# First block of x in column slices, each turned on TensorE just ahead of its products

## The chip, the cores and the metric

One core of one Trainium2 chip. The metric is the device time of one execution in microseconds (us). The kernel before took 542.69 us (median of 3 runs, 542.49 to 542.8). The question of the whole document is about the first 35 us of it: what follows is not touched by the change.

Names: TensorE (PE in the profile, with its weight loads as PEld), VectorE (DVE), ScalarE (ACT), GpSimd (POOL), SyncE's queue of transfers (SPq). "Turn" means a 128x128 transpose on TensorE through the identity matrix. Where turns stand between products, a "turn" is one call of `turn`: eight such transposes in the kernel before, four in the changed one. "Eviction" is the copy of a finished PSUM bank to SBUF. At "half pace" a matmul of 512 columns starts 0.427 us after the one before it instead of 0.216 (both in the profile of the kernel before); "release" is the moment when half pace ends. A "filler" is a matmul of zeros whose result nobody uses.

## The reference

```python
B, S, Dm, Df = 1, 2048, 1024, 3584          # all bf16
g = einsum("bsd,df->bsf", x, w_gate)
u = einsum("bsd,df->bsf", x, w_up)
h = gelu(g) * u                             # tanh form
out = einsum("bsf,fd->bsd", h, w_down)
```

## The kernel before

The kernel keeps x transposed (`xT`, k on the partitions) in blocks of 512 rows, handles two blocks per pass, and multiplies 256 columns of `w_gate` and `w_up` at a time. For most of its length it uses seven products instead of eight per pair of blocks, made from sums and differences of tiles: `s` of weights, `t` of `xT`. VectorE makes the first of these. Only the first block (block 0) of the first pass with the first 256 weight columns is multiplied plainly, while `s` and `t` do not exist yet. The change touches this beginning alone.

How block 0 is loaded and turned, and the order of the transfers, all of them on one queue:

```python
def load_x(c):                       # four tiles of 128 rows, 2048-byte rows
    for i in range(NS):              # NS = 4
        xn = slot([P, Dm], bf16, "xn")
        nc.sync.dma_start(out=xn, in_=x2[r0 : r0 + P, :])
...
def turn(xT, xn, c, i, copy):        # 8 transposes into one bank, one eviction
    tp = bank[4 + i].bitcast(bf16).rearrange("p (k r) -> p k r", k=NKB)
    for ko in range(NKB):            # NKB = 8
        nc.tensor.transpose(tp[:, ko, :], xn[i][:, ko * P : (ko + 1) * P], ident)
    copy(out=xT[c][:, :, i * P : (i + 1) * P], in_=tp)
...
xn0 = load_x(0)
for k0, k1 in ((0, 2), (2, 5), (5, NKB)):
    load_wf(nc.sync, k0, k1)         # first weights, gate then up, three parts
w = load_w(1)                        # next weights, gate then up
for ko in range(NKB):
    transposing(xT, 1, ko, N)        # second block, transposed by the transfer
ahead = load_w(2)
```

What the engines do with it:

```python
keep_warm(NWARM, N)                  # 5 matmuls of zeros, 512 columns
for i in range(NS):
    if i > 0:
        keep_warm(3, 2 * P)          # 3 fillers of 256 columns
    turn(xT, xn0, 0, i, on_act if i == 1 else on_dve)
plain(bank[0:4], 0, range(0, 2), parts=2)
plain(bank[0:4], 0, range(2, NKB))   # pairs of k-blocks: per pair, bank by bank
s["s1"] = s["how"]["s1"](s, range(1))
finish(bank[0:4], 0)                 # twice: h = gelu(gate bank) * up bank
s["s1"] += s["how"]["s1"](s, range(1, 2))
nxt = {"p1": first_product(odd, xT, w)}
s.make("sa", "s2", "s3", "s4")       # VectorE goes on without a pause ...
t.make("t1")                         # ... into the differences of xT
```

`plain` makes four results (gate and up, twice 128 columns) in four PSUM banks. It takes two k-blocks for one bank, then two for the next. `finish` needs a Gelu on ScalarE and a product `hT` on VectorE for each half.

## Time and profile before

| what | value | where it is read |
|---|---|---|
| time (median), span of the profiled run (which took 542.47 us) | 542.69 us, 540.6 us | times, page |
| TensorE busy | 535.9 us, 99% | page, part 1 |
| first turn, first product | 3.53, 7.18 us | timeline |
| first chunk (block 0) ends | 14.18 us | records of single matmuls |
| VectorE's second `hT` product starts | 14.57 us | timeline |
| last TensorE wait for VectorE | 29.15 us | timeline |

From the page of the kernel before: the span, the busy line of TensorE (busy us, share, instructions) and the chain that ended last.

```profile
span 540.6 us, 7439 instructions
PE 535.9 (99%) x2414; PEld 378.8 (70%) x2414; DVE 341.4 (63%) x526; ACT 258.7 (48%) x463; POOL 236.4 (44%) x213
...
PE 99%; ACT 0%; DVE 0%; issue 0%
```

The timeline of the kernel before, with lines left out. Columns: start in us, duration in us, engine, line, operation, output<-inputs, shape, count, and in brackets the idle time before it and what ended that.

```profile
1.19 2.31 PE L501 MATMUL bank<-warm 128*128 128x512 bf16 x5 [1.19 <-DVE warm L432]
...
3.53 1.03 PE L448 MATMUL bank<-ident,xn 128*128 128x128 bf16 x8
4.35 0.85 PE L501 MATMUL bank<-warm 128*128 128x256 bf16 x3
4.99 0.80 PE L448 MATMUL bank<-ident,xn 128*128 128x128 bf16 x8
...
6.74 0.61 PE L448 MATMUL bank<-ident,xn 128*128 128x128 bf16 x8
7.18 17.52 PE L111 MATMUL bank<-xT,w 128*128 128x256 bf16 x88
...
13.08 0.60 ACT L179 ACTIVATE g<-bank 128x512 f32<-128x512 f32 x1 [4.93 <-PE bank L111]
13.71 0.69 DVE L90 TENSOR_TENSOR hT<-g,bank 128x512 bf16<-128x512 f32 x1 [1.02 <-ACT g L179]
13.94 0.60 ACT L179 ACTIVATE g<-bank 128x512 f32<-128x512 f32 x1 [0.27 <-PE bank L111]
14.57 0.69 DVE L90 TENSOR_TENSOR hT<-g,bank 128x512 bf16<-128x512 f32 x1 [0.18 <-ACT g L179]
15.18 0.68 DVE L90 TENSOR_TENSOR s<-w 128x512 fp32r<-128x512 bf16 x1
```

Two things to see. The turns at 3.53 take 1.03 us for eight, those at 6.74 take 0.61: TensorE runs at half pace until about 5.4 us. And from 15.18 on VectorE's lines have no bracket, so it never waits again in this stretch; each of its instructions starts when the one before lets it.

The same timeline further on: TensorE's last waits in this kernel that VectorE ends.

```profile
27.34 1.46 PEld L111 LDWEIGHTS bank<-t,s 128*128 128x128 f32 x7 [0.31 <-DVE hT L90]
27.80 1.29 DVE L90 TENSOR_TENSOR t<-xT 128x512 fp32r<-128x512 bf16 x2
...
29.15 0.99 PEld L111 LDWEIGHTS bank<-t,s 128*128 128x128 f32 x5 [0.35 <-DVE t L90]
```

The two differences `t` started at 27.80 end at 29.09, and TensorE goes on at 29.15. After that it has no wait that matters: whatever the beginning gains or loses by here stays to the end.

### The profile page before, as it was taken

To read this page: it belongs to the slowest core of one execution; us is meant where nothing else is said; L and a number is where in the kernel's file an instruction comes from. 1 tells how busy PE (TensorE), PEld (TensorE's weight loads), DVE (VectorE), ACT (ScalarE), POOL (GpSimd) and SP (SyncE) were. 2 spreads that over 40 slices of the span, in tenths; PEclk is the share of its full clock that TensorE was granted. 3 is DMA by queue.
4 is the path that set the end of the run, shared out by engine and by line. 5 is a ranking of instruction groups with operands and counts; after the bars stand their busy time and mean duration, and the time that the engine had idled before them with its cause. 6 is when DMAs were issued, how large, how long until landed. Compare 5 with 4: busy or idle time off the path is not lost.

```text
span 540.6 us, 7439 instructions
## 1 busy us (share of the span) xinstructions
PE 535.9 (99%) x2414; PEld 378.8 (70%) x2414; DVE 341.4 (63%) x526; ACT 258.7 (48%) x463; POOL 236.4 (44%) x213
## 2 busy tenths in 40 slices
PE   9999999999999999999999999999999999999997
PEld 5567777667766646888876776677777775488885
DVE  2986666776666895694945545555544559676730
ACT  2566666566665410255355555555555541114431
POOL 0069966677774400000097777777766600000000
PEclk9999999999999999999999999999999999999999
DMA  9776666666654899979672222222331069363751
GB/s 245 152 187 176 175 183 203 190 185 199 200 165 171 269 381 313 295 189 294 230 194 79 78 79 78 79 78 80 84 100 50 1 196 384 140 236 95 231 188 49
DMA packets 108133, 93.28 MB, mean 173 GB/s; under 512 B 17216, under 2 KB 92992, under 8 KB 108096
## 3 DMA queue, kind: packets, MB, share of 16 engines
q1 hardware_dynamic: 108096, 92.82, 59.2%
q8 instruction: 19, 0.31, 0.3%
q14 instruction: 18, 0.15, 0.1%
HBM read 74.45 MB, written 15.20 MB: 166 GB/s over the span
## 4 chain that ended last, share of the span: by engine, by line
PE 99%; ACT 0%; DVE 0%; issue 0%
PE bank L111 98%; PE bank L501 1%; PE bank L448 0%; ACT st L412 0%; DVE warm L432 0%
## 5 line engine op out<-in xcount | busy, mean ns | idle before, releaser
L93 POOL TENSOR_TENSOR s<-w 128x512 fp32r<-128x512 bf16 x100 | 116.9, 1189 | 154.9 <-PE bank L111 154.9
L111 PE MATMUL bank<-t,s 128*128 128x512 f32 x648 | 157.4, 398 | 0.0
L111 PEld LDWEIGHTS bank<-t,s 128*128 128x128 f32 x648 | 121.6, 188 | 28.2 <-DVE t L90 0.3
L111 PE MATMUL bank<-xT,w 128*128 128x512 bf16 (+1 forms) x504 | 116.2, 377 | 0.0
L107 ACT COPY p<-bank 128x512 f32<-128x512 f32 x124 | 70.5, 591 | 94.0 <-PE bank L111 94.0
L90 DVE TENSOR_TENSOR hT<-g,bank 128x512 bf16<-128x512 f32 x112 | 76.6, 687 | 55.1 <-ACT g L179 49.5
L111 PEld LDWEIGHTS <-w 128*128 128x128 bf16 x504 | 45.1, 98 | 59.0 <-issue 13.4
L90 DVE TENSOR_TENSOR sum<-bank,p 128x512 f32<-128x512 f32 x54 | 37.4, 692 | 52.6 <-PE bank L111 50.9
L179 ACT ACTIVATE g<-sum 128x512 f32<-128x512 f32 x81 | 51.5, 636 | 34.5 <-DVE sum L90 33.6
L111 PE MATMUL bank<-q 128*128 128x512 f32 x240 | 58.9, 389 | 0.0
L111 PE MATMUL bank<-t,sa 128*128 128x512 f32 x216 | 58.6, 413 | 0.0
L93 POOL TENSOR_TENSOR s<-w,s 128x512 fp32r<-128x512 bf16 x50 | 57.7, 1175 | 0.0
L93 POOL TENSOR_TENSOR s<-s,w 128x512 fp32r<-128x512 f32 x50 | 57.0, 1161 | 0.0
L111 PE MATMUL bank<-tb,s 128*128 128x512 f32 x216 | 53.3, 389 | 0.0
L111 PEld LDWEIGHTS bank<-q 128*128 128x128 f32 x240 | 45.1, 188 | 9.3
L111 PE MATMUL bank<-raw,hT 128*128 128x512 bf16 x224 | 48.7, 379 | 0.0
L111 PEld LDWEIGHTS bank<-t,sa 128*128 128x128 f32 x216 | 40.7, 188 | 10.6
L111 PEld LDWEIGHTS bank<-tb,s 128*128 128x128 f32 x216 | 40.6, 188 | 8.4
L102 ACT CAST tb<-raw 128x512 fp32r<-128x512 bf16 x28 | 17.2, 626 | 59.6 <-DMA raw<-in_w_down_dram 24.2
L107 ACT COPY u<-bank 128x512 f32<-128x512 f32 x62 | 35.9, 590 | 19.7 <-PE bank L111 19.7
L90 DVE TENSOR_TENSOR bank<-bank,p 128x512 f32<-128x512 f32 x54 | 37.8, 700 | 8.9 <-PE bank L111 5.8
L90 DVE TENSOR_TENSOR q<-hT 128x512 fp32r<-128x512 bf16 x56 | 38.5, 687 | 4.7 <-PE bank L111 4.7
(45 smaller groups left out, 444.7 us busy)
## 6 DMA issues: line engine op xcount, KB each, us to landing
raw<-in_w_down_dram SPq DMA_DIRECT2D x80, 256.0 KB, 4.8
q<-td SPq DMA_DIRECT2D x60, 256.0 KB, 5.0
w<-in_w_gate_dram SPq DMA_DIRECT2D x27, 512.0 KB, 5.9
w<-in_w_up_dram SPq DMA_DIRECT2D x27, 512.0 KB, 7.0
td<-m SPq DMA_DIRECT2D x12, 768.0 KB, 4.6
w<-td SPq DMA_DIRECT2D x6, 1024.0 KB, 9.5
out_dram<-st SPq DMA_DIRECT2D x32, 128.0 KB, 1.7
td<-w SPq DMA_DIRECT2D x2, 768.0 KB, 7.0
```

The source lines that it names most:

```text
L90: nc.vector.tensor_tensor(out=out, in0=a, in1=b, op=op)
L93: nc.gpsimd.tensor_tensor(out=out, in0=a, in1=b, op=op)
L102: nc.scalar.copy(out=t, in_=src)
L107: nc.scalar.copy(out=t, in_=ps)
L111: nc.tensor.matmul(ps, lhsT=lhs, rhs=rhs, start=start, stop=stop, skip_group_check=True)
L179: nc.scalar.activation(g, src, ACT.Gelu_apprx_tanh)
L501: nc.tensor.matmul(bank[3][:, :cols], lhsT=warm[:, :P], rhs=warm[:, :cols], start=True, stop=True)
```

## The change

Intent: do not wait for the whole of block 0. Load it in four slices of 256 columns (two k-blocks each, 512-byte rows), put the first weights between the slices, and turn each k-block just ahead of the four matmuls that use it. Those matmuls keep TensorE busy, so the fillers go.

```diff
-    def load_x(c):  ... out=xn, in_=x2[r0 : r0 + P, :]
+    def load_x(q):
+        xn = slot([P, NS, 2 * P], bf16, "xn")
+        cols = x2[:N, 2 * q * P : 2 * (q + 1) * P]
+        nc.sync.dma_start(out=xn, in_=cols.rearrange("(i p) c -> p i c", p=P))
+        return xn
+
+    def turn(k):
+        tp = bank[4 + k % 4].bitcast(bf16)[:, :N]
         for i in range(NS):
-    ... 8 transposes of one row tile, eviction of 128x1024 by VectorE or ScalarE
+            nc.tensor.transpose(tp[:, i * P : (i + 1) * P],
+                xn0[k // 2][:, i, k % 2 * P : (k % 2 + 1) * P], ident)
+        nc.vector.tensor_copy(out=xT[0][:, k, :], in_=tp)
...
+    ORDER_0 = "T0 T1 M0 M1 T2 T3 M2 T4 M3 T5 M4 T6 M5 T7 M6 M7"   # turns, products
-    xn0 = load_x(0)
-    for k0, k1 in ((0, 2), (2, 5), (5, NKB)):
-        load_wf(nc.sync, k0, k1)
+    xn0 = [load_x(0)]
+    load_wf(0, 2)
+    xn0.append(load_x(1))
+    load_wf(2, 5)
+    xn0 += [load_x(2), load_x(3)]
+    load_wf(5, NKB)
...
-        keep_warm(NWARM, N)
-        for i in range(NS):
-            if i > 0:
-                keep_warm(3, 2 * P)
-            turn(xT, xn0, 0, i, on_act if i == 1 else on_dve)
-        plain(bank[0:4], 0, range(0, 2), parts=2)
-        plain(bank[0:4], 0, range(2, NKB))
+        for _ in range(NWARM):
+            nc.tensor.matmul(bank[3], lhsT=warm[:, :P], rhs=warm, start=True, stop=True)
+        for what, k in ORDER_0:
+            if what == "T":
+                turn(k)
+            else:
+                plain(bank[0:4], 0, [k])        # one k-block over the four banks
```

More of the change, by code (lines that the diff above doesn't have):

```diff
@@ L434 @@
     make_identity(nc, ident)
-    def load_x(c):
-        t = []
-        for i in range(NS):
-            xn = slot([P, Dm], bf16, "xn")
-            r0 = c * N + i * P
-            nc.sync.dma_start(out=xn, in_=x2[r0 : r0 + P, :])
-            t.append(xn)
-        return t
-    def turn(xT, xn, c, i, copy):
-        tp = bank[4 + i].bitcast(bf16).rearrange("p (k r) -> p k r", k=NKB)
-        for ko in range(NKB):
-            nc.tensor.transpose(tp[:, ko, :], xn[i][:, ko * P : (ko + 1) * P], ident)
-        copy(out=xT[c][:, :, i * P : (i + 1) * P], in_=tp)
+    def load_x(q):
[5 more added lines that the diff above has]
+        tp = bank[4 + k % 4].bitcast(bf16)[:, :N]
+        for i in range(NS):
+            nc.tensor.transpose(
+                tp[:, i * P : (i + 1) * P],
+                xn0[k // 2][:, i, k % 2 * P : (k % 2 + 1) * P],
+                ident,
+            )
+        nc.vector.tensor_copy(out=xT[0][:, k, :], in_=tp)
     def transposing(xT, c, ko, r0):
@@ L454, in transposing, with load_wf @@
         )
-    def load_wf(queue, k0, k1):
+    def load_wf(k0, k1):
         for i, src in enumerate((w_gate, w_up)):
-            got = queue.dma_start(
+            nc.sync.dma_start(
                 out=wf[:, i, k0:k1],
@@ L463, in load_wf @@
             )
-            if queue is not nc.sync:
-                tc.keep_in_program_order(got)
+    ORDER_0 = [(step[0], int(step[1])) for step in "T0 T1 M0 M1 T2 T3 M2 T4 M3 T5 M4 T6 M5 T7 M6 M7".split()]
     xT = new_x()
-    xn0 = load_x(0)
     wf = wpool.tile([P, 2, NKB, 2 * P], bf16, name="w")
-    for k0, k1 in ((0, 2), (2, 5), (5, NKB)):
-        load_wf(nc.sync, k0, k1)
+    xn0 = [load_x(0)]
[4 more added lines that the diff above has]
+    load_wf(5, NKB)
     w = load_w(1)
@@ L475, with plain @@
     ahead = load_w(2)
-    def plain(ps, c, kos, parts=1):
-        n = N // parts
-        for k in range(kos.start, kos.stop, 2):
-            for part in range(parts):
-                cols = slice(part * n, (part + 1) * n)
-                for p, (j, i) in zip(ps, [(j, i) for j in range(2) for i in range(2)]):
-                    for ko in (k, k + 1):
-                        matmul(
-                            p[:, cols],
-                            wf[:, i, ko, j * P : (j + 1) * P],
-                            xT[c][:, ko, cols],
-                            ko == 0 and part == 0,
-                            ko == NKB - 1,
-                        )
+    def plain(ps, c, kos):
+        for p, (j, i) in zip(ps, [(j, i) for j in range(2) for i in range(2)]):
+            for ko in kos:
+                matmul(
+                    p,
+                    wf[:, i, ko, j * P : (j + 1) * P],
+                    xT[c][:, ko, :],
+                    ko == 0,
+                    ko == NKB - 1,
+                )
     def finish(ps, c):
@@ L494, in finish @@
             times(j, c, gelu(ps[2 * j]), ps[2 * j + 1])
-    on_dve, on_act = nc.vector.tensor_copy, nc.scalar.copy
     s, t = sums_s(w, dve), sums_t(xT)
     with tc.manual_schedule(engines={ENG.Activation}):
-        def keep_warm(n, cols):
-            for _ in range(n):
-                nc.tensor.matmul(
-                    bank[3][:, :cols], lhsT=warm[:, :P], rhs=warm[:, :cols], start=True, stop=True
-                )
-        keep_warm(NWARM, N)
-        for i in range(NS):
-            if i > 0:
-                keep_warm(3, 2 * P)
-            turn(xT, xn0, 0, i, on_act if i == 1 else on_dve)
-        plain(bank[0:4], 0, range(0, 2), parts=2)
-        plain(bank[0:4], 0, range(2, NKB))
+        for _ in range(NWARM):
[5 more added lines that the diff above has]
+                plain(bank[0:4], 0, [k])
         s["s1"] = s["how"]["s1"](s, range(1))
@@ L522, in rest_of_0 @@
         if part == 0:
-            plain(bank[4:8], 1, range(NKB))
+            for k in range(0, NKB, 2):
+                plain(bank[4:8], 1, (k, k + 1))
             t.make("t2", "tb")
```

## The prediction

> **What bounds the kernel now.** TensorE: busy 535.9 of 540.6 us, 99% of the chain that ended last. In the timeline no gap over 0.1 us follows about 29.5 us, so the change can only win what TensorE is ahead when that steady stream starts. Before it:
>
> - Weights and x share one DMA stream: by the windows view about 310 GB/s from 2 to 8 us.
> - The timeline has warm-up matmuls from 1.19 us, four turns of x between 3.53 and 7.18 with filler matmuls between them, then the first products, gapless from 7.18 to 14.18.
> - VectorE is full (windows view: 2.00 of every 2 us) from 15.2 to 35 us. TensorE waits for it at 27.35 and 29.15 (a difference tile "t" that ended at 29.10). That second wait is the last one: VectorE's chain sets the start of the steady stream.
> - The DMA-transposed rows of the second x block land at about 18.45 (4th) up to 22.82 us (8th); TensorE first uses the 8th at 23.03. Slack 0.2 us.
>
> **Removed.** 9 filler matmuls (3 x 0.32 cold, 6 x 0.11 warm, 1.6 us), one ScalarE copy (1.01 us) and an activation-table load, and the wait for all of x before the first product.
>
> **Added and moved.** Transposes stay 32 (0.107 us apart cold, 0.055 warm). VectorE evicts 8 times 128x512 instead of 3 times 128x1024 (0.69 each); my estimate from that duration is 0.40 each. The first product needs slice 0, the first weights and an eviction: estimated 4.7-4.9 us instead of 7.2. But products now wait for data: two turns then their product leaves an eviction gap of about 0.45 us near 7 us, and the fifth product waits for the last weights. Product time itself (32 x 0.216 = 6.9 us) is unchanged.
>
> Slices have 512-byte rows, not 2048. In the DMA packet records of this trace a 512 B packet takes 27 ns and a 2048 B one 84 ns: 19 against 24 GB/s per engine. [...]this trace shows it is slower than 2 KB. Estimate: x takes 0.5 us longer, so the last weights land near 10.7 (10.2 before), and everything queued behind, including the 8th transposed row (to about 23.3), is later by up to 0.5.
>
> So the eight steps end at about 13.8 instead of 14.18: 0.4 us. Then the gain goes: all four banks now finish within the last 0.86 us, so Gelu of bank 0 (0.60) holds the next product by 0.2, and both Gelus run after it, so VectorE's second h product starts near 14.6, as before (14.58). Its full chain then ends as before, and the transposed rows cap TensorE as well. **Little or nothing remains at 29 us.**
>
> **Risk.** [...] Here half pace lasts to about 5.4 us. [...]
>
> **Predicted: 542.8 us, range 541.9 to 544.3.** Faster by over 2%: 1%; within 2%: 98%; slower: 1%.
>
> **Right if:** first product near 4.8, first chunk done 13.5-14.0, VectorE's chain from 15.2 unchanged within 0.3 us, TensorE after 30 us shifted under 0.3 us. **Wrong if:** matmuls keep a 0.43 us pitch past 6 us (clock; slower), or the second x block lands at the old times and the head gains over 0.7 us (then up to 0.5 faster), or slices land more than 1 us late.

The forecast's sum: 0.4 us gained at the end of the chunk (13.8 instead of 14.18), all of it lost again to the late Gelus, so about the time of the kernel before, 542.8 us. Beside the sum stood a risk term, one chance in four that half pace lasts longer without fillers and the beginning loses time. The range, up to 544.3, leaves room for it; the sum does not hold it.

## The result, and the profile after

The changed kernel took 543.62 us (median of 4 runs, 542.74 to 544.72), the kernel before 542.75 us (4 runs, 542.49 to 542.87). The ratio is 1.0018, with a 95% interval of 0.9994 to 1.0041: the same within 2%, and not clear of noise. Here and below a ratio is the mean time of one kernel's runs over that of the other's runs of the same rounds, so it is not quite the ratio of the medians.

The four times are two pairs: 542.74 and 542.86, 544.37 and 544.72. The profile is of the slowest of them. Its page:

```profile
span 542.9 us, 7407 instructions
PE 537.2 (99%) x2397; PEld 377.5 (70%) x2397; DVE 342.7 (63%) x531; ACT 256.1 (47%) x461; POOL 236.9 (44%) x213
...
PE 98%; DMA 1%; DVE 1%; SPq 0%; ACT 0%; issue 0%
```

The timeline of the changed kernel, same columns, lines left out:

```profile
3.63 1.03 PE L445 MATMUL bank<-ident,xn 128*128 128x128 bf16 x8
...
4.75 0.59 PE L111 MATMUL bank<-xT,w 128*128 128x512 bf16 x1
...
5.99 3.17 PE L111 MATMUL bank<-xT,w 128*128 128x512 bf16 x7 [0.65 <-DMA w<-in_w_up_dram]
...
8.95 1.06 PE L445 MATMUL bank<-ident,xn 128*128 128x128 bf16 x8
...
10.10 1.02 PE L111 MATMUL bank<-xT,w 128*128 128x512 bf16 x4
...
14.44 12.45 PE L111 MATMUL bank<-xT,w 128*128 128x512 bf16 x56
...
15.72 1.09 ACT L179 ACTIVATE g<-bank 128x512 f32<-128x512 f32 x2 [13.71 <-PE bank L111]
16.35 1.28 DVE L90 TENSOR_TENSOR hT<-g,bank 128x512 bf16<-128x512 f32 x2 [0.69 <-PE bank L111]
17.55 0.69 DVE L90 TENSOR_TENSOR s<-w 128x512 fp32r<-128x512 bf16 x1
```

The first product starts 2.4 us sooner than before (4.75 against 7.18), does one matmul, and then TensorE stands until the first up weights have landed at 5.95 us (landing records). The seven matmuls from 5.99 take 3.17 us and the eight turns from 8.95 take 1.06: half pace still, where before it had ended at 5.4. The four matmuls at 10.10 are the first at full pace (0.215 us from start to start). The first chunk ends at 16.17 us, and the second `hT` product, the second of the pair that starts at 16.35, starts at 16.96 in the records instead of 14.58.

Further on the changed kernel shows the same two lines as before, 2.4 us later. Nothing between 15 and 31 us has taken back or added anything:

```profile
30.18 1.29 DVE L90 TENSOR_TENSOR t<-xT 128x512 fp32r<-128x512 bf16 x2
...
31.52 0.99 PEld L111 LDWEIGHTS bank<-t,s 128*128 128x128 f32 x5 [0.33 <-DVE t L90]
```

**Where the head start went, in TensorE's time.** The 32 products take 6.9 us at full pace in both kernels. In this profile 4.75 + 6.9 would be 11.65. To that come 2.47 us because the first eight products took from 4.75 to 8.95 (half pace and the wait for up weights) instead of 1.73; 0.85 for two turns at half pace and 0.89 for four at full pace, all of which now stand between products; and 0.30 for an eviction ahead of the third product. The sum is 16.16, the measured end 16.17.

**A rule that the profiles obey.** The span follows the start of VectorE's second `hT` product. Span minus that start is 526.0 us before (540.57 - 14.58) and 526.0 after (542.94 - 16.96). The experiments add twelve more profiles: eleven lie between 525.9 and 526.1, and one, at 526.3, is told below.

**The clock's own record.** Each trace also keeps, though no view prints it, when the full clock was granted to TensorE: from 5.38 us in the kernel before, from 10.10 in the changed kernel. The grant lasts 535.892 us before and 532.479 us after. In the profiles of the experiments it begins anywhere from 3.92 us (experiment 11) to 9.2 us (experiment 1). What sets its beginning, the traces do not show.

### The profile page after: what moved, and what is told of

It is laid out like the page before. It is cut to its first block, busy times and chain, and to the rows that moved or that the text cites. A ratio compares the mean times of both kernels' runs of the same rounds, so it can differ in the third digit from the quotient of the medians.

```text
span 542.9 us, 7407 instructions
## 1 busy us (share of the span) xinstructions
PE 537.2 (99%) x2397; PEld 377.5 (70%) x2397; DVE 342.7 (63%) x531; ACT 256.1 (47%) x461; POOL 236.9 (44%) x213
## 4 chain that ended last, share of the span: by engine, by line
PE 98%; DMA 1%; DVE 1%; SPq 0%; ACT 0%; issue 0%
PE bank L111 97%; DMA w<-in_w_up_dram 1%; PE bank L445 0%; DVE t L90 0%; DVE bank L90 0%; DVE hT L90 0%; ACT st L412 0%; SPq L459 0%; SPq L439 0%; DVE xT L450 0%
## 5 line engine op out<-in xcount | busy, mean ns | idle before, releaser
L111 PE MATMUL bank<-xT,w 128*128 128x512 bf16 x496 | 118.9, 384 | 0.9 <-DMA w<-in_w_up_dram 0.7
```

Of the source, the lines that this page charges most:

```text
L111: nc.tensor.matmul(ps, lhsT=lhs, rhs=rhs, start=start, stop=stop, skip_group_check=True)
```

## The experiments

Two theories for the two groups of times. *Theory A (clock)*: TensorE starts at half pace, and in some runs of the changed kernel the release comes late, as in its profile (10.10 us against 5.38), because TensorE now stands waiting in that stretch. *Theory B (loads)*: the slow runs are those whose first weights land late, whatever the pace. Beside these stand the smaller claims of the prediction: short rows, the late Gelus, the cap by the second block.

Kernels 1 to 4 ran on one chip, 5 to 8 on a second, 9 to 12 on a third, each with its own runs of the kernel before: medians 542.84 (11 runs, 542.3 to 543.38), 542.61 (11 runs, 542.3 to 543.48) and 542.96 (9 runs, 542.08 to 543.16).

### 1. The changed kernel again

No edit.

> The changed kernel once more, unedited, to see whether its times really fall into two groups (542.74 and 542.86 against 544.37 and 544.72). Theory A (clock): TensorE stays at half pace (0.43 us from one 512-column matmul to the next) until about 10 us in the slow runs[...]; expect two groups again, about 542.8 and 544.5, and in the profile a half pace to about 10 us if the profiled run is over 544, to about 5.4 to 6.8 us if it is under 543. Theory B (loads): the slow runs are those in which the first weights land late (5.95 us in the profile of after); expect two groups that follow the landing of the first up weights, at whatever clock.

Measured: 542.63, 542.92, 543.09 and 544.46, 544.57, 544.77; ratio 1.0013 (0.9999 to 1.0026). Two groups again. Of the ten runs of the changed kernel so far five average 542.85 and five 544.58, which is 1.73 us apart. All ten average 543.71, the 15 runs of the kernel before beside them 542.80, so the mean loss of 0.9 us is that of the slow group. The profile fell on a run of 544.57: half pace until 9.2 us, up weights landed at 5.85 us, second `hT` at 16.78. Both theories expected two groups. Both slow profiles have the late landing and the late release together, so this run does not part the theories.

### 2. Fillers ahead of the first product

```diff
+                if k == 0:
+                    for _ in range(6):
+                        nc.tensor.matmul(bank[3][:, :256], lhsT=warm[:, :P],
+                            rhs=warm[:, :256], start=True, stop=True)
                 plain(bank[0:4], 0, [k])
```

> The changed kernel with six filler matmuls of 256 columns between the first two turns and the first product, about 1.3 us at half pace. Theory A (clock): release near 5.4 us in every run, one group at 542.4 to 542.9, none over 543.2. Theory B (loads): the weights land as late as without fillers, so two groups remain, 542.8 and 544.5.

Measured: 543.13 to 543.79 in five runs, ratio 1.0012 (1.0 to 1.0024). One group, so the slow one is gone, as theory A said, though fillers cannot bring weights sooner. The level that theory A gave, 542.4 to 542.9, was missed by 0.7 us: the fillers themselves hold the first product until 5.79 us, and in this profile the release came only at about 6.9 us.

### 3. The kernel before without its fillers

```diff
         for i in range(NS):
-            if i > 0:
-                keep_warm(3, 2 * P)
             turn(xT, xn0, 0, i, on_act if i == 1 else on_dve)
```

> The kernel before without its nine filler matmuls between the turns, nothing else. Theory A (clock): the first products start at half pace in some or all runs; release moves from 5.4 us to as late as about 10 us, and the time rises by 0.5 to 1.7 us, to 543.2 to 544.4. Theory B (loads): fillers do not matter, 542.4 to 542.9.

Measured: 542.21 us, 541.79 to 542.35, ratio 0.9987 (0.9975 to 0.9999). Neither theory had expected it to be faster. Timeline of this kernel:

```profile
3.49 3.54 PE L448 MATMUL bank<-ident,xn 128*128 128x128 bf16 x32
...
6.87 10.40 PE L111 MATMUL bank<-xT,w 128*128 128x256 bf16 x54
```

The 32 turns run back to back, 3.5 to 6.87, all but the last at 0.107 us from one to the next, that is at half pace, and the first product behind them runs at full pace. The grant of the full clock begins at 6.84, after 3.35 us of nothing but transposes (the five warm-up matmuls end at 3.50). Without the fillers the first product starts 0.3 us sooner than before. Experiment 9 repeats this kernel.

### 4. The kernel before with x in column slices

```diff
-            xn = slot([P, Dm], bf16, "xn")
-            nc.sync.dma_start(out=xn, in_=x2[r0 : r0 + P, :])
+            xn = slot([P, NS, 2 * P], bf16, "xn")
+            cols = x2[:N, 2 * q * P : 2 * (q + 1) * P]
+            nc.sync.dma_start(out=xn, in_=cols.rearrange("(i p) c -> p i c", p=P))
```

(All four slices ahead of all weights, turned slice by slice, fillers kept.)

> The kernel before with x loaded in four slices of 256 columns (512-byte rows) ahead of all weights, turned slice by slice with the fillers kept: the cost of the short rows alone. By the prediction the last of the first weights lands about 0.5 us later than 10.2 us and the 8th transposed row about 0.5 us later than 22.8; TensorE's slack there was 0.2 us, so the time should be 542.7 to 543.3. If the short rows cost nothing, 542.5 to 542.9 and unchanged landings.

Measured: 543.25 us, 542.86 to 543.35, ratio 1.0005 (0.9993 to 1.0017). In the timing alone this is not clear of noise. In the profile the first up weights land at 8.01 us (7.32 before), the last of the first weights at 10.72 (10.20 before), and the first product starts at 7.61 (7.18 before); the second `hT` follows at 15.17, 0.59 later. The eighth row of the second block lands at 22.87 against 22.82. The short rows thus cost about half a microsecond between these two profiles, as predicted, but through the first weights and not through the second block. The sign is safer than the size: in the five profiles with the loads of the kernel before (before, experiments 3, 5, 9 and 12) the first up weights land anywhere from 6.67 to 7.80 us and the last first weights from 9.74 to 10.46, and experiment 4 is later than all five.

### 5. The kernel before with its last k-blocks one by one

```diff
-        plain(bank[0:4], 0, range(2, NKB))
+        plain(bank[0:4], 0, range(2, 6))
+        for ko in (6, 7):
+            for p, (j, i) in zip(bank[0:4], [(j, i) for j in range(2) for i in range(2)]):
+                matmul(p, wf[:, i, ko, j * P : (j + 1) * P], xT[0][:, ko, :],
+                       False, ko == NKB - 1)
```

> The kernel before, with the last two of its eight k-blocks of the first chunk done one by one over the four banks instead of as a pair per bank; same loads, same matmuls. The Gelu theory of the prediction: the banks then finish within 0.86 us instead of 1.5, both Gelus (0.60 each) follow the last products, and VectorE's second h product starts about 0.8 us after the chunk's end instead of 0.4; the time rises by 0.3 to 0.4 us, to about 543.1 to 543.3. Rival (TensorE alone counts): the chunk ends at the same moment, so no change, within 0.1 us of before.

Measured: 543.16 us, 542.58 to 543.46, ratio 1.0009 (0.9996 to 1.0022). Timing again leans the expected way without being clear. The profile decides: the chunk ended at 13.87 us, and the second `hT`, the second of the two below, started at 14.66, which is 0.79 later. Before it was 14.58 - 14.18 = 0.40.

```profile
13.42 1.08 ACT L179 ACTIVATE g<-bank 128x512 f32<-128x512 f32 x2 [5.58 <-PE bank L111]
14.05 1.28 DVE L90 TENSOR_TENSOR hT<-g,bank 128x512 bf16<-128x512 f32 x2 [1.45 <-PE bank L111]
```

The two Gelus run as one stretch because both banks were ready, where before there was a pause of 0.27 us between them that TensorE ended. Banks that finish together cost 0.39 us against banks that finish in turn. The span sides with VectorE and not with TensorE: the chunk ended 0.30 us sooner than in the profile before, the second `hT` started 0.08 later, and the span is 0.12 longer (540.69 against 540.57).

### 6. Fillers inside the wait

```diff
+            if n == 1:                       # after the first matmul of M0
+                for _ in range(fill):        # fill = 4 for M0, else 0
+                    nc.tensor.matmul(bank[3][:, :256], lhsT=warm[:, :P],
+                        rhs=warm[:, :256], start=True, stop=True)
```

> The changed kernel with four fillers of 256 columns placed after the first matmul of the first product, where TensorE waits for the first up weights anyway. Theory A (clock): the slow group near 544.5 vanishes and, unlike the fillers ahead of the product (543.1 to 543.8), nothing useful is delayed: 542.6 to 543.2 in every run, half pace ending by 7 us. Theory B (loads): still two groups, 542.8 and 544.5.

Measured: 543.02 to 543.42 in five runs, ratio 1.0008 (0.9996 to 1.002). One group, 0.2 us above the range in its slowest run.

```profile
4.56 0.58 PE L111 MATMUL bank<-xT,w 128*128 128x512 bf16 x1
4.94 1.06 PE L485 MATMUL bank<-warm 128*128 128x256 bf16 x4
5.80 1.86 PE L111 MATMUL bank<-xT,w 128*128 128x512 bf16 x7
7.50 0.61 PE L445 MATMUL bank<-ident,xn 128*128 128x128 bf16 x8
...
8.40 1.02 PE L111 MATMUL bank<-xT,w 128*128 128x512 bf16 x4 [0.29 <-DVE xT L450]
```

Seven matmuls in 1.86 us, where the slow profile needed 3.17. Half pace ends at about 6.2 us. The sum for this profile: 4.56 + 6.9 for the products, + 1.21 (first eight products 4.56 to 7.50), + 1.34 for six turns between products, + 0.45 of eviction wait ahead of the line at 8.40, is 14.46; the chunk ended at 14.47, and the second `hT` started 0.79 later at 15.26. So even with the pace released in time the chunk ends 0.29 us later than in the profile before, and the late banks add 0.39.

### 7. The changed kernel with its last two products paired

```diff
-    ORDER_0 = "... T6 M5 T7 M6 M7"
+    ORDER_0 = "... T6 M5 T7 M6"           # M6 now does k-blocks (6, 7) bank by bank
```

> The changed kernel with its last two products done as a pair per bank, as the kernel before does. Gelu theory: VectorE's second h product comes 0.4 us instead of 0.8 us after the chunk's end, so both groups move down by 0.3 to 0.4 us: about 542.4 and 544.1. Rival (TensorE alone counts): both groups unchanged.

Measured: 542.71, 542.76, 542.92, 543.73, 544.81, 544.98; ratio 1.0017 (1.0002 to 1.0032). The lower group did not move down. The profiled run (542.92, released at about 6.4 us, up weights landed at 4.94) shows why:

```profile
12.57 0.38 PE L111 MATMUL bank<-xT,w 128*128 128x512 bf16 x1
12.77 0.42 DVE L450 COPY xT<-bank 128x512 bf16<-128x512 bf16 x1 [0.66 <-PE bank L445]
...
13.24 4.04 PE L111 MATMUL bank<-xT,w 128*128 128x512 bf16 x18 [0.30 <-DVE xT L450]
```

The pair needs the eighth turn at once, and its eviction ends at 13.19. TensorE loses 0.46 us (13.24 - 12.57 - 0.216, rounded). The second `hT` now follows the chunk's end by 0.40 (15.15 - 14.75) as the Gelu theory says, but that end is later. The mend traded one wait for another.

### 8. Both mends, and gate products first

```diff
-    zip(ps, [(j, i) for j in range(2) for i in range(2)])
+    zip([ps[n] for n in (0, 2, 1, 3)], [(j, i) for i in range(2) for j in range(2)])
+    # three fillers behind the two gate matmuls of M0; M6 = k-blocks (6, 7)
```

> The changed kernel with both mends, and both gate products ahead of both up products so that useful work and three fillers bridge the wait for the first up weights. If clock and Gelu are the two losses beside the short rows: one group, 542.1 to 542.7. If something else holds the slow runs: two groups, and no run under 542.5.

Measured: 542.73 to 543.76 in five runs, ratio 1.0011 (0.9999 to 1.0023). No run near 544.5 (up weights had landed as late as 5.58 us in the profile), but not the level hoped for: the wait of 0.46 us at 13.18 is here too, and the second `hT` starts at 15.14. The five runs still part in two, 542.73 and 542.93 against 543.51 to 543.76, and none is under 542.5, which is what the expectation had given for "something else". The profile fell on a run of 542.93, so what holds the other three stays open.

### 9. The kernel before without fillers, again

No edit against experiment 3, another chip.

> The kernel before without its nine fillers once more, unedited, on whatever chip this is, to see whether the first result (542.21, range 541.79 to 542.35, against 542.84) holds. Expected 0.3 to 0.6 us under before; theory: the fillers sit in front of turns whose x has already landed, so they delay the first product[...]. Rival: the first result was a lucky chip or lucky loads; then within 0.15 us of before.

Measured: 542.72, 542.79, 542.9, 543.99, 544.02; ratio 1.0008 (0.9996 to 1.0021). The gain of experiment 3 did not hold: two of the five runs are a microsecond slower than the rest, which no run of the kernel before, with fillers, ever was (35 runs, 542.08 to 543.48). In the profile, which fell on one of the faster runs, TensorE waited 1.01 us for the third row tile, which landed at 6.17 us (5.12 in experiment 3). Whether the two slow runs were released late was not profiled; it is what theory A had foretold for experiment 3 ("543.2 to 544.4").

### 10. All mends, eighth turn moved ahead

```diff
-    ORDER_0 = "... T6 M5 T7 M6"
+    ORDER_0 = "... T6 T7 M5 M6"
```

> The changed kernel with gate products first, three fillers in the wait for the first up weights, the last two products as a pair per bank, and the eighth turn moved ahead of the sixth product, so that the pair no longer waits 0.46 us for the eviction of that turn. Theory: the second h product moves from about 15.15 to about 14.7 us, so 542.3 to 542.9 in one group, about equal to before. Rival (short rows and their late loads set the end): unchanged from the version without this move, 542.7 to 543.8.

Measured: 542.6 us, 542.34 to 543.04, ratio 0.9997 (0.9984 to 1.0009). The time is as expected: the chunk ends at 14.04 us and the second `hT` starts at 14.49. In this profile half pace had ended by 4.7 us, before the fillers. Here the beginning is 0.1 us ahead of the kernel before, and the cap of the prediction shows, in this one of the 14 profiles alone:

```profile
23.66 1.67 PE L111 MATMUL bank<-xT,w 128*128 128x512 bf16 x7 [0.61 <-DMA xT<-in_x_dram]
```

The eighth transposed row landed at 23.62 us, and TensorE lost 0.77 us there (0.99 us from one matmul to the next instead of 0.216); 0.3 of it was left when the steady stream began. This is the profile in which span minus second `hT` is 526.3.

### 11. Two halves instead of four slices

```diff
-    NWARM = 5
+    NWARM = 7
+    # load_x(q), q in 0..1: two tiles of 256 rows x 512 columns (1024-byte rows)
-    load_x(0), wf(0, 2), load_x(1), wf(2, 5), load_x(2), load_x(3), wf(5, 8)
+    load_x(0), wf(0, 2), load_x(1), wf(2, 5), wf(5, 8)
-    "T0 T1 M0 M1 T2 T3 M2 T4 M3 T5 M4 T6 M5 T7 M6 M7"      # one k-block each
+    "T0 T1 T2 T3 M0 T4 T5 T6 T7 M2 M4 M6"                   # pairs of k-blocks
```

> The idea of the change with two halves of 512 columns (1024-byte rows) instead of four slices, seven warm-up matmuls that reach the landing of the first half, four turns ahead of the first pair of products and four behind it, all products as pairs per bank. [...]chunk ends near 13.5, second h product near 13.9 to 14.1, time 541.7 to 542.2, faster than before and than before without fillers. If shorter rows alone spoil it: 542.6 to 543.2.

Measured: 542.59 us, 542.36 to 542.68, ratio 0.9995 (0.9981 to 1.0008). The first forecast took the clock, eviction waits and late banks for the losses. Slower than hoped, and at the lower edge of what the expectation gave for short rows alone. The pace was released at about 3.9 us, so the clock cost nothing, but TensorE stood for the first up weights:

```profile
5.48 0.60 PE L111 MATMUL bank<-xT,w 128*128 128x512 bf16 x2 [0.23 <-DMA w<-in_w_gate_dram]
6.80 1.47 PE L111 MATMUL bank<-xT,w 128*128 128x512 bf16 x6 [0.72 <-DMA w<-in_w_up_dram]
```

They landed at 6.76 us. The second `hT` starts at 14.74.

### 12. No fillers and no warm-up matmuls

```diff
-    NWARM = 5
+    NWARM = 0            # on top of experiment 3
```

> The kernel before without fillers and without its five warm-up matmuls, so that only transposes (from 3.5 us) precede the products. If transposes count as work for the clock: [...]times between 542.0 and 543.9, spread. If they do not count: [...]543.7 to 544.5.

Measured: 542.61 to 543.52 in five runs, ratio 1.0004 (0.9991 to 1.0016). Half pace ended at about 7.5 us, 0.36 us into the products, after nothing but transposes and a wait of 0.20 us from 3.39 to 7.15. All five times lie in the range given for transposes that count.

No version beat both kernels beyond doubt: experiments 10 and 11 lie at ratios 0.9997 and 0.9995 to before, with intervals that include 1, and experiment 3 did not repeat.

## Why the prediction was right or wrong

**The time, and "little or nothing remains": right.** Predicted 542.8 us with a range of 541.9 to 544.3, measured 543.62. That median lies between the two groups and no run took it: two of the four runs match the 542.8, the other two, 544.37 and 544.72, lie above the range. The faster half of the runs averages 542.85, the kernel before 542.75. One figure on the way was wrong: the nine fillers took 1.3 us in the records (3 x 0.213 and 6 x 0.109), not 1.6.

**The clock: half pace did last longer in some runs, probably more often than foreseen.** The prediction gave this, as the author's estimate, one chance in four (the passage is cut). The changed kernel and its paired variant, neither with fillers, ran 16 times, and 7 of the runs are at 544.37 or more. The four variants with fillers (experiments 2, 6, 8, 10) ran 20 times, and none is over 543.79. The two groups of the changed kernel lie 1.73 us apart. Against the well-released profile of experiment 6 the slow profile's chunk ends 1.70 us later, made of 1.26 more for the first eight products, 0.41 more for two turns at half pace, 0.19 of later start, and 0.16 less of eviction wait. The releases, from 3.92 us (experiment 11) to 10.10 us (after), stand at no fixed place from the start of the kernel.

**Theory B falls as a sole cause.** Up weights that landed late, at 5.72 us (experiment 10) and 5.58 us (experiments 2 and 8), did not make a run over 544, while in the slow profiles they landed at 5.85 and 5.95 us. But only filled kernels were caught with such landings and a good time. In the profile of the changed kernel TensorE stands 0.65 us for the up weights, and half pace lasts to 10.10 us. In experiment 6, with fillers in that wait, half pace ended at 6.17; in experiment 7, without fillers and with up weights that landed at 4.94, it ended at 6.35. That a late landing and the clock make the loss together fits these profiles, but how they do it was not shown. How often the weights land late stays open: no fast run of the unedited changed kernel was profiled.

**Half pace behind transposes: it ended.** In experiment 3 it ended at 6.84 us after 3.35 us of transposes alone, in experiment 12 at about 7.5 us after transposes from 3.39 us on and 0.36 us of products.

**The chunk's end "about 13.8": too early, by 0.2 to 0.7 us even in released runs.** It was 14.47 in experiment 6, which has fillers in the way, and 14.75 in experiment 7, of which 0.46 is that variant's own wait. For the unprofiled fast runs of the changed kernel an estimate is their span (540.8 to 541.3 us in five runs) less 526.0 and less 0.79: 14.0 to 14.5. The term that was too small is the first eight products: they took 2.93 us in experiment 6 and 2.59 in experiment 7, where the prediction's dates (first product near 4.8, the gap behind the next two turns near 7) leave about 1.8. Half pace lasted into them, to 6.17 and 6.35 us. The loads also ran behind the estimate of 10.7 us for the last of the first weights, which landed at 11.38 in the changed kernel and at 11.03 in experiment 6, but in both profiles TensorE waits for no load after the first up weights, so this did not move the chunk's end.

**Gelu at the end: right.** The first Gelu holds the next product by 0.20 us (16.37 - 15.95 - 0.216), as predicted, and it is 0.79 us from the chunk's end to the second `hT` in the changed kernel and in experiments 5 and 6, 0.40 in the kernel before and in experiment 7. The prediction's end of chunk at 13.8 and `hT` "near 14.6" have the same distance.

**VectorE's chain sets the rest: right, and firmer than predicted.** Span minus second `hT` is 526.0 us within 0.1 in 13 of 14 profiles, over a range of 14.27 to 16.96 for that start. "VectorE's chain from 15.2 unchanged within 0.3 us" itself failed in the profiled run, where the chain starts 2.4 us later: 1.7 for the clock, and by experiment 6 0.3 for the chunk's end and 0.4 for the late banks. A profile is one run, though: the 35 runs of the kernel before spread over 1.4 us, and its profile is of a fast one, so differences of 0.3 us between two profiles are sizes in these runs and not averages.

**The second block as a cap: not binding in the changed kernel.** Its eighth row landed at 23.32 us, as predicted (23.3), though 24.08 in experiment 1, and by then TensorE itself was later. The cap is real: experiment 10 met it and lost 0.3 us to it.

**Short rows: the size was about right in the one profile.** Experiment 4's profile, against that of the kernel before, puts them at 0.4 us for the first product and 0.6 for the second `hT`; its timing, 1.0005 (0.9993 to 1.0017), allows anything from nothing to 0.9 us.

## What to carry to other kernels

An earlier first product is worth only what the last link of the start-up gets. Find that link (here one VectorE product whose start plus 526 us was the span) and follow the change to it through every term: turns that move into the chain, evictions, banks that finish together. When matmuls of zeros are removed because real work will replace them, check that the real work has no waits while TensorE is still at half pace. In the changed kernel's profile it waited there 0.65 us, and half pace lasted to 10.10 us instead of 5.38; the changed kernel and its paired variant, without fillers, took 544.37 us or more in 7 of 16 runs, the variants with fillers over 543.79 in none of 20. Repeated runs then show two groups where one profile shows only one of them.

## What else the traces showed

- In experiment 3 only transposes ran from 3.5 us, and half pace ended at 6.84 us; in experiment 12, without any matmul before them, at about 7.5 us.
- In the packet records of the first 12 us of the kernel before a 512 B packet takes 27 ns and a 2048 B one 84 ns (medians), 19 against 24 GB/s per engine, and with x in 512-byte rows the first up weights landed at 8.01 us (experiment 4) against 6.67 to 7.80 in the five profiles with 2048-byte rows.
- The sixteen shares of one transfer land apart: 4.14 and 5.85 us, first and last, for the first up weights in experiment 1, but 3.92 and 4.72 in experiment 6. In the profile of the changed kernel the first share itself came only at 4.89 us, the last at 5.95, and TensorE went on at 5.99, behind the last. So the spread is not the whole of the delay. The cause stays open.
